# A list scheduler that ranks operations by their own index, against one that passes over the program forwards and backwards

## The chip, the cores and the metric

The kernel runs on one core of one Trainium2 chip. The metric is the device time of one execution in microseconds (us), the median of several runs. The core has five engines that each run their own instructions in the order in which the program issues them: TensorE (PE, matrix multiplies; its weight loads show as PEld), VectorE (DVE), ScalarE (ACT), GpSimd (POOL) and SyncE (SP, which here only issues DMA transfers). They wait for each other by semaphores.

## What is computed

Top-k attention over 4 batches of 8 heads (576 tokens, 64 columns a head), followed by two feed-forward stages on the 2304 tokens:

```python
scores = scale * np.matmul(q, k.transpose(0, 1, 3, 2))
kth = np.partition(scores, -top_k, axis=-1)[..., -top_k:-top_k + 1]   # top_k = 32
scores = np.where(scores >= kth, scores, -1000000000.0)
attn = np.exp(scores - np.max(scores, axis=-1, keepdims=True))
attn = attn / (np.sum(attn, axis=-1, keepdims=True) + 1e-09)
x = np.matmul(attn, v)            # then heads beside each other: 2304 x 512
h = x @ w_in                      # 512 -> 2048
x = (h * (1.0 / (1.0 + np.exp(-h)))) @ w_out
x = ((x @ w1) * (x @ w2) @ w3) @ w_out2   # 512 -> 1024 -> 1024 -> 512
```

## The kernel before

The tokens are worked in six blocks of 384 (three tiles of 128 each). For a block, attention goes head by head. PE makes the scores (`bank<-kk,qs`), ACT copies them out of the PSUM bank (`st<-bank`), DVE finds the 32 largest of each row in four rounds of `max` with three of `match_replace` between them (`top<-wk`, `wk<-top`), ACT masks and exponentiates (`e<-st,top`, `e<-e,nb`), DVE makes the reciprocal of the sum (`rc`), POOL multiplies (`e<-e,rc`), PE transposes (`bank<-ident,e`; in block 0 it multiplies by a diagonal instead, `dg`), ACT copies (`pn`, `pf`, `ph`), and PE multiplies with the values (`pn,vn`, `ph,vt`, `pl,vt`). When the eight heads of a block are done, its feed-forward work follows on PE: `xh,wt` and `gh,wt` with their low halves `xl` and `gl`, `x2h,wt`, and at the end `w4h,gh`. A matrix product in high precision is made of three PE products, since each operand is split into a rounded high half (ACT) and a rest (POOL subtracts). The gate of the first stage goes `th` (ACT), `gf` (DVE), `gh` (ACT), `gl` (POOL). All eight PSUM banks are one pool with the tag `bank`.

While block 0 and its feed-forward stage run, the weights are made ready: SP loads 48 pieces of 512 KB (`raw`), ACT, POOL and DVE unpack them (`t`, `bank<-raw,low`, `w`), ACT and POOL split them (`wt<-w`, `wt<-w,wt`), and ACT stores them to a scratch tensor in memory (`scr<-wt`), from which later blocks read them (`wt<-scr`). Ahead of that w3 and the last weight are multiplied with each other ("fold", `bank<-w`, `bank<-w4r,w`), so that one product is left of the two.

The order of the instructions is not written out. Every call is recorded as an `Op` with what it needs; `Op.cost` gives each a modelled time on its engine (`hold`) and until its result is there (`done`), in ns. `Recorder.schedule` then lets the five engines run in that model: whenever an engine is free it takes, among the operations whose inputs and buffers are there, the one with the lowest index in the recorded program. Sorted by the modelled start, the calls are issued by `emit` (L356 in the profile: all engine instructions have this one line, so the rows are read by their tiles). Buffers of a pool are handed out in the recorded order of their first use.

Of the kernel before, what the change touches and what calls it, by code (L numbers as in the profile page):

```python
# [2 lines left out]

# [11 lines left out]
I16 = mybir.dt.int16  # L15
# [124 lines left out]
class Op:  # L140
# [63 lines left out]
class Recorder:  # L204
# [52 lines left out]
    def schedule(self):  # L257
        ops = self.ops
        left, heirs, weak = [len(o.needs) + len(o.weak) for o in ops], [[] for _ in ops], [[] for _ in ops]
        users, ahead, turn = {}, {}, {}  # L260
        for n, o in enumerate(ops):
            for k in sorted(o.needs):
                heirs[k].append(n)
            for k in sorted(o.weak):
                weak[k].append(n)
            for t in o.tiles:
                users[t] = users.get(t, 0) + 1
            for t in o.takes:
                turn[t] = ahead[t.key] = ahead.get(t.key, -1) + 1
        spare = {k: [(0., c) for c in range(v)] for k, v in self.caps.items()}  # L270
        given, lastuse, parked = {}, {}, {}
        avail, start = [0.] * len(ops), [0.] * len(ops)
        ready = {e: [] for e in ("sync", "scalar", "vector", "gpsimd", "tensor")}
        later = {e: [] for e in ready}
        free = dict.fromkeys(ready, 0.)
        wire = busy = held = 0.
        reserved = {}

        def offer(n):
            o = ops[n]  # L280
            for t in o.takes:
                if t in reserved:
                    continue
                if given.get(t.key, 0) != turn[t] or not spare[t.key]:
                    parked.setdefault(t.key, []).append(n)
                    return
            for t in o.takes:
                if t not in reserved:
                    reserved[t] = heapq.heappop(spare[t.key])
                    given[t.key] = given.get(t.key, 0) + 1  # L290
                avail[n] = max(avail[n], reserved[t][0])
            heapq.heappush(later[o.engine], (avail[n], n))
            for t in o.takes:
                wake(t.key)

        def wake(key):
            for n in parked.pop(key, []):
                offer(n)

        for n in range(len(ops)):  # L300
            if not left[n]:
                offer(n)
        for _ in ops:
            best = None
            for e in ready:
                if ready[e] or later[e]:
                    t = free[e] if ready[e] else max(free[e], later[e][0][0])
                    if best is None or t < best[0]:
                        best = t, e
            t, e = best  # L310
            while later[e] and later[e][0][0] <= t:
                heapq.heappush(ready[e], heapq.heappop(later[e])[1])
            n = heapq.heappop(ready[e])
            o = ops[n]
            late = 0.
            if o.shares and busy > t + AVOID:
                aside = [n]
                while ready[e] and ops[ready[e][0]].shares:
                    aside.append(heapq.heappop(ready[e]))
                n = heapq.heappop(ready[e]) if ready[e] else aside.pop(0)  # L320
                for x in aside:
                    heapq.heappush(ready[e], x)
                o = ops[n]
            if o.shares:
                late = max(0., busy - t)
                held = t + late + o.hold
            elif e == "gpsimd":
                late = max(0., held - t)
                busy = t + late + o.hold
            start[n] = t  # L330
            free[e] = t + late + o.hold
            end = t + late + o.done
            if o.dma:
                wire = max(wire, t + 1400) + o.done
                end = wire + 1050
            for x in o.tiles:
                users[x] -= 1
                lastuse[x] = max(lastuse.get(x, 0.), end + 45)
                if not users[x]:
                    heapq.heappush(spare[x.key], (lastuse[x], reserved[x][1]))  # L340
                    wake(x.key)
            for k in heirs[n]:
                left[k] -= 1
                same = e == "tensor" and ops[k].engine == e
                avail[k] = max(avail[k], free[e] if same else end + 45)
                if not left[k]:
                    offer(k)
            for k in weak[n]:
                left[k] -= 1
                if not left[k]:  # L350
                    offer(k)
        return [ops[n] for n in sorted(range(len(ops)), key=lambda n: (start[n], n))]

    def emit(self):
        for o in self.schedule():
# [4 lines left out]
def attention_moe_moe2_kernel(  # L360
# [839 lines left out]
```

## Time and profile before

| | |
|---|---|
| median of 3 runs | 1139.78 us (1139.05 to 1140.88) |
| the profiled execution's own time | 1139.82 us |
| its span, first to last instruction | 1138.0 us |
| PE busy | 1081.0 us (95%) |
| DVE, ACT, POOL busy | 903.2, 854.9, 745.3 us |
| mean granted clock of TensorE | 0.983 of 2.4 GHz |

The span is what the trace covers; 1.8 us of the execution's time lie around it. Busy time is the union of an engine's instructions. The granted clock has two levels here, 1.0 (2.4 GHz) and 0.5 (1.2 GHz); a mean between them says how much of a stretch stood at each.

### The profile page before, as it was taken

Reading aid. Unit: us, or ns where it says so; the run is one execution under the profiler, and the core shown is the slowest. Engines: PE = TensorE matmul, PEld = TensorE weight load, DVE = VectorE, ACT = ScalarE, POOL = GpSimd, SP = SyncE. Lnnn points to the kernel's source line nnn. Section 1 sums busy time; section 2 is a strip of 40 time slices with the busy share of each in tenths; the row PEclk is TensorE's granted clock in tenths of the full one; section 3 lists DMA queues with packets and bytes.
Section 4 is the critical chain, followed back from the end, with each engine's and each line's share of the span. In section 5 each row is a group of like instructions: output and inputs, shape, how many; then the busy total and the mean of one; then the engine's idle time right before and its main releaser. Section 6 shows DMA issues by size and latency. Waiting matters only on the chain.

```text
span 1138.0 us, 19557 instructions
## 1 busy us (share of the span) xinstructions
PE 1081.0 (95%) x6096; PEld 986.9 (87%) x6096; DVE 903.2 (79%) x2062; ACT 854.9 (75%) x1911; POOL 745.3 (65%) x766
## 2 busy tenths in 40 slices
PE   3899977988899999999999999999999999999998
PEld 2555557888898999999999999999999999999997
DVE  7999899897989999998999888888899999401100
ACT  5999699898787778878887887888787778542221
POOL 3778458888786567777777866777766677542221
PEclk8999998999899999999999999999999999999999
DMA  8896389999988776767778667888757765448740
GB/s 263 263 288 197 114 271 308 313 324 315 313 290 290 231 238 216 238 205 231 253 259 292 222 200 275 272 306 296 253 171 254 252 226 192 136 158 259 254 146 29
DMA packets 127880, 273.54 MB, mean 240 GB/s; under 512 B 40480, under 2 KB 65056, under 8 KB 127776
## 3 DMA queue, kind: packets, MB, share of 16 engines
q1 hardware_dynamic: 119712, 245.02, 66.6%
q10 hardware_dynamic: 8064, 27.27, 6.2%
q8 instruction: 49, 0.80, 0.3%
q14 instruction: 55, 0.45, 0.1%
HBM read 216.14 MB, written 56.10 MB: 239 GB/s over the span
## 4 chain that ended last, share of the span: by engine, by line
PE 79%; ACT 7%; DVE 6%; POOL 3%; issue 3%; DMA 2%; ACTq 0%; SPq 0%; POOLq 0%; DVEq 0%
PE bank L356 79%; DVE top L356 3%; DVE wk L356 2%; ACT e L356 2%; POOL gl L356 1%; ACT t L356 1%; ACT st L356 1%; DVE w L356 1%; ACT wt L356 1%; ACT bank L356 1%; POOL wt L356 1%; ACT pn L356 1%; DMA raw<-in_w_dram 1%; DMA kk<-k 0%; DMA wt<-scr 0%
## 5 line engine op out<-in xcount | busy, mean ns | idle before, releaser
L356 DVE MAX8 top<-wk 128x8 f32<-128x576 f32 x432 | 319.9, 753 | 5.3
L356 POOL TENSOR_TENSOR gl<-gf,gh 128x384 fp32r<-128x384 f32 x144 | 147.2, 1022 | 158.8 <-ACT gh L356 157.6
L356 PE MATMUL bank<-xh,wt 128*128 128x384 f32 x768 | 225.0, 344 | 7.7 <-ACT st L356 7.0
L356 PE MATMUL bank<-gh,wt 128*128 128x384 f32 x768 | 224.9, 343 | 3.7 <-ACT gh L356 3.5
L356 PE MATMUL bank<-x2h,wt 128*128 128x384 f32 x768 | 221.7, 344 | 0.2 <-ACT x2h L356 0.2
L356 DVE MATCH_REPLACE8 wk<-top,wk 128x576 f32<-128x576 f32 x288 | 213.3, 742 | 0.0
L356 PE MATMUL bank<-kk,qs 128*128 128x288 f32 x640 | 150.8, 322 | 21.8 <-ACT kk L356 15.2
L356 ACT ACTIVATE st<-bank 128x288 f32<-128x288 f32 (+1 forms) x320 | 129.3, 411 | 39.8 <-PE bank L356 36.7
L356 POOL TENSOR_TENSOR pl<-pf,ph 128x384 fp32r<-128x384 f32 x128 | 129.5, 1018 | 38.0 <-ACT ph L356 35.8
L356 PEld LDWEIGHTS bank<-kk,qs 128*128 128x128 f32 x640 | 116.3, 195 | 41.1 <-issue 18.6
L356 PEld LDWEIGHTS bank<-xh,wt 128*128 128x128 f32 x768 | 142.9, 190 | 10.1 <-ACT st L356 7.7
L356 PEld LDWEIGHTS bank<-gh,wt 128*128 128x128 f32 x768 | 141.4, 190 | 5.1 <-ACT gh L356 4.7
L356 PEld LDWEIGHTS bank<-x2h,wt 128*128 128x128 f32 x768 | 141.6, 189 | 2.6 <-ACT x2h L356 0.8
L356 PE MATMUL bank<-gl,wt 128*128 128x384 f32 x384 | 131.4, 342 | 2.4 <-POOL gl L356 1.9
L356 DVE MAX8 top<-st 128x8 f32<-128x576 f32 x144 | 108.0, 752 | 29.2 <-ACT st L356 28.4
L356 PE MATMUL bank<-xl,wt 128*128 128x384 f32 x384 | 130.5, 340 | 0.0
L356 PE MATMUL bank<-x2l,wt 128*128 128x384 f32 x384 | 129.9, 339 | 0.1
L356 POOL TENSOR_SCALAR e<-e,rc 128x640 f32<-128x640 f32 (+1 forms) x120 | 95.6, 805 | 35.5 <-DVE rc L356 32.9
L356 ACT CAST gh<-gf 128x384 fp32r<-128x384 f32 x144 | 74.1, 515 | 52.7 <-DVE gf L356 51.5
L356 ACT ACTIVATE e<-st,top 128x576 f32<-128x576 f32 x144 | 107.4, 778 | 6.6 <-DVE top L356 5.3
L356 ACT ACTIVATE e<-e,nb 128x576 f32<-128x576 f32 x144 | 111.6, 777 | 0.0
L356 DVE SCALAR_TENSOR_TENSOR gf<-th,bank 128x384 f32<-128x384 f32 x96 | 52.5, 547 | 74.2 <-ACT th L356 72.5
(82 smaller groups left out, 2333.1 us busy)
## 6 DMA issues: line engine op xcount, KB each, us to landing
wt<-scr SPq DMA_DIRECT2D x240, 512.0 KB, 4.2
scr<-wt ACTq DMA_DIRECT2D x48, 512.0 KB, 5.3
k<-kk SPq DMA_DIRECT2D x32, 576.0 KB, 4.2
kk<-k SPq DMA_DIRECT2D x32, 576.0 KB, 5.0
raw<-in_w_dram SPq DMA_DIRECT2D x24, 512.0 KB, 5.7
kr<-in_kT_dram SPq DMA_DIRECT2D x32, 288.0 KB, 4.8
raw<-in_w3T_dram SPq DMA_DIRECT2D x16, 512.0 KB, 5.1
raw<-in_w_in_dram SPq DMA_DIRECT2D x16, 512.0 KB, 6.0
```

Source lines behind the costliest of these rows:

```text
L356: o.call(*[real_ap(x) for x in o.args], **{k: real_ap(x) for k, x in o.kw.items()})
```

## The change

Three things are different; the operations, their number and their sizes are not.

The times in `Op.cost` are set anew for a few kinds: matmuls 2 ns longer or 14 ns shorter, POOL's multiply and subtract by other straight lines, ACT's copies that don't read a bank 29 ns longer. The delay from a result to the instruction that waits for it, 45 ns for all before, is 17 to 70 ns by the waiting engine (`WAKE`).

The forward pass takes a rank in place of the recorded index. `backward` runs the same model from the end: an operation may start (backwards) when all that use its result have, buffers are taken at their last use and come free at their first, and the modelled place from the end is the new rank, so that an operation that may run late has a high one.

`schedule` begins with the recorded index as the rank, and then makes 24 rounds of two passes each, forwards and backwards, with durations that are disturbed at random by up to 5% (transfers by up to 15%). It keeps the rank whose forward passes in three fixed sets of disturbed durations have the least modelled end. The last forward pass uses the plain durations.

```diff
+ROUNDS = 24
+CASES = 3
+ENGINES = ("sync", "scalar", "vector", "gpsimd", "tensor")
+WAKE = (17, 24, 24, 70, 44)
+POOL, PE = 3, 4
...
-                t = max(m / 2.4 * 13 / 12, 110)
+                t = max(m / 2.4 * 13 / 12 + 2, 110)
-                t = 108 if self.name == "transpose" else m / 0.6 + (100 if columns(src) < 128 else 20)
+                t = 108 if self.name == "transpose" else m / 0.6 + (100 if columns(src) < 128 else 6)
...
-                t = 740 if src.dtype == I16 else max(360, n * 1.14 + 45)
+                t = 740 if src.dtype == I16 else n * 0.85 + 236
             else:
-                t = n * 2.42 + 46
+                t = n * 2.16 + 146 if n > 64 else 300
         if self.name == "copy":
-            t = n / 0.96 - 24
+            t = n / 0.96 + (-24 if in_bank(self.ins) else 5)
...
+    def forward(self, rank, hold, done):
+        ops, engine = self.ops, self.engine
+        left = [len(o.needs) + len(o.weak) for o in ops]
+        offer, back, pick, avail, free = self.queues(rank, self.takes, self.turn, left, lambda n: 0.)
+        users, lastuse = [len(u) for u in self.users], [0.] * len(self.key)
+        start, total = [0.] * len(ops), 0.
+        wire = busy = held = 0.
+            t, e, ready = pick()
+            n = heapq.heappop(ready)[1]
...
+            total = max(total, end)
...
+        return start, total
+
+    def backward(self, start, hold, done):
+        ops, engine = self.ops, self.engine
+        last = [max(u, key=lambda n: (start[n], n)) for u in self.users]
+        left = [len(h) for h in self.heirs]
+        takes, before, turn, seen = [[] for _ in ops], [[] for _ in ops], [0] * len(last), {}
+        for t in sorted(range(len(last)), key=lambda t: (-start[last[t]], -last[t], t)):
+            turn[t] = seen[self.key[t]] = seen.get(self.key[t], -1) + 1
+            takes[last[t]].append(t)
...
+        rank = [-(start[n] + hold[n]) for n in range(len(ops))]
+        offer, back, pick, avail, free = self.queues(rank, takes, turn, left, lambda n: done[n] - hold[n] + 45)
+        users, firstuse = [len(u) for u in self.users], [0.] * len(last)
+        begin, wire = [0.] * len(ops), 0.
+        for _ in ops:
+            t, e, ready = pick()
+            n = heapq.heappop(ready)[1]
+            free[e] = t + hold[n]
+            u = t + hold[n]
+            if ops[n].dma:
+                wire = max(wire, t) + done[n]
+                u = max(u, wire + 1400)
+            begin[n] = -u
...
+            for k in self.needs[n]:
+                left[k] -= 1
+                gap = 1050 if ops[k].dma else done[k] - hold[k]
+                avail[k] = max(avail[k], free[e] if e == PE and engine[k] == PE else u + gap + self.wake[n])
...
+        return begin
+
+    def jitter(self, dice, amount):
+        hold, done = [], []
+        for o in self.ops:
+            f = 1. + amount * (2. * dice.random() - 1.)
+            hold.append(o.hold if o.dma else o.hold * f + (0. if o.engine == "tensor" else 8.))
+            done.append(o.done * (1. + 3. * amount * dice.random()) if o.dma else o.done * f + 8.)
+        return hold, done
+
+    def schedule(self):
+        self.graph()
+        dice = random.Random(7)
+        cases = [self.jitter(dice, 0.04) for _ in range(CASES)]
+
+        def cost(rank):
+            return sum(self.forward(rank, *c)[1] for c in cases)
+
+        rank = list(range(len(self.ops)))
+        least = cost(rank)
+        for _ in range(ROUNDS):
+            times = self.jitter(dice, dice.choice((0., 0.02, 0.05)))
+            r = rank
+            for _ in range(2):
+                r = self.backward(self.forward(r, *times)[0], *times)
+                c = cost(r)
+                if c < least:
+                    least, rank = c, r
+        start, _ = self.forward(rank, [o.hold for o in self.ops], [o.done for o in self.ops])
+        return [self.ops[n] for n in sorted(range(len(start)), key=lambda n: (start[n], n))]
```

The instructions of an engine stay close to where they were: at the same place stand 4054 of PE's 5792, 837 of ACT's 1822, 702 of DVE's 1630, 327 of POOL's 758 and 355 of SP's 650; the mean distance is 2.1 places on PE and ACT, 1.4 on DVE and POOL, 0.9 on SP, and it is largest in the first third. Three places are shown, with the buffers' numbers, which differ between the two programs.

The first is ACT in the feed-forward stage of block 0, where the gate of its first piece of 128 columns goes from `th` to `gh` (`th_1881`, `gh_1924` before; `th_1838`, `gh_1863` after). Before:

```order
L356 ACTIVATE th_1881<-bank_1777 128x384
L356 DMA scr4_96<-wt_1851 128x1024
L356 ACTIVATE t_1885<-raw_1654 128x512
L356 ACTIVATE bank_1891<-raw_1654,low_90 128x512
L356 CAST wt_1899<-w_1807 128x512
L356 ACTIVATE t_1905<-raw_1682 128x512
L356 CAST wt_1911<-w_1871 128x512
L356 ACTIVATE st_1813<-bank_1819 64x288
L356 CAST qs_1915<-qr_1796 128x384
L356 CAST kk_1919<-kr_1856 128x576
L356 DMA scr5_97<-wt_1899 128x1024
L356 CAST gh_1924<-gf_1889 128x384
```

After:

```order
L457 ACTIVATE th_1838<-bank_1780 128x384
L457 ACTIVATE bank_1844<-raw_1639,low_90 128x512
L457 ACTIVATE st_1697<-bank_1765 128x288
L457 ACTIVATE st_1859<-bank_1822 128x288
L457 CAST gh_1863<-gf_1847 128x384
```

Before, ten instructions stood between the two (unpacking, splitting and storing of weights, a copy of scores, the casts `qs` and `kk` of a later head); now three do, a step of unpacking and two copies of scores.

The second is POOL a little ahead of it, where the low half of a head's queries is made (`qs_1775` before, `qs_1770` after, the sixth row and the last). Before:

```order
L356 TENSOR_TENSOR wt_1652<-w_1585,wt_1652 128x512
L356 TENSOR_SCALAR t_1665<-t_1665 128x512
L356 TENSOR_TENSOR wt_1687<-w_1614,wt_1687 128x512
L356 TENSOR_SCALAR t_1721<-t_1721 128x512
L356 TENSOR_TENSOR wt_1729<-w_1658,wt_1729 128x512
L356 TENSOR_TENSOR qs_1775<-qr_1551,qs_1775 64x384
L356 TENSOR_SCALAR e_1746<-e_1746,rc_1772 128x576
L356 TENSOR_SCALAR e_1750<-e_1750,rc_1772 128x576
L356 TENSOR_TENSOR kk_1780<-kr_1573,kk_1780 128x576
L356 TENSOR_TENSOR xl_1847<-xf_1693,xh_1802 128x384
L356 TENSOR_SCALAR t_1830<-t_1830 128x512
L356 TENSOR_TENSOR wt_1851<-w_1691,wt_1851 128x512
```

After:

```order
L457 TENSOR_TENSOR xl_1663<-xf_1364,xh_1657 128x384
L457 TENSOR_SCALAR dg_1468<-ident_89,rc_1655 128x128 x2
L457 TENSOR_SCALAR t_1674<-t_1674 128x512
L457 TENSOR_SCALAR t_1718<-t_1718 128x512
L457 TENSOR_TENSOR wt_1734<-w_1641,wt_1734 128x512
L457 TENSOR_TENSOR wt_1744<-w_1711,wt_1744 128x512
L457 TENSOR_SCALAR t_1748<-t_1748 128x512
L457 TENSOR_TENSOR kk_1758<-kr_1636,kk_1758 128x576
L457 TENSOR_TENSOR xl_1794<-xf_1691,xh_1785 128x384
L457 TENSOR_TENSOR qs_1770<-qr_1497,qs_1770 64x384
```

The subtraction for `qs` has moved behind those for a later `kk`, `xl`, a `t` and a `wt`, which followed it before; the two multiplications `e` that came right after it have gone further back too.

The third is the end of the program on PE. `bank_14016`, `bank_14024` and `bank_14032` collect the last block's three output tiles in this order, and each is copied out by ACT when its last product is done. Before, the last nine products:

```order
L356 MATMUL bank_14016<-w4h_87,gh_14289 128x512
L356 MATMUL bank_14016<-w4l_88,gh_14289 128x512
L356 MATMUL bank_14016<-w4h_87,gl_14293 128x512
L356 MATMUL bank_14024<-w4h_87,gh_14289 128x512
L356 MATMUL bank_14024<-w4l_88,gh_14289 128x512
L356 MATMUL bank_14024<-w4h_87,gl_14293 128x512
L356 MATMUL bank_14032<-w4h_87,gh_14289 128x512
L356 MATMUL bank_14032<-w4l_88,gh_14289 128x512
L356 MATMUL bank_14032<-w4h_87,gl_14293 128x512
```

After, rows up to six ahead of the end:

```order
L457 MATMUL bank_14016<-w4h_87,gh_14280 128x512
L457 MATMUL bank_14016<-w4l_88,gh_14280 128x512
L457 MATMUL bank_14016<-w4h_87,gl_14284 128x512
L457 MATMUL bank_14032<-w4h_87,gh_14203 128x512
L457 MATMUL bank_14032<-w4l_88,gh_14203 128x512
L457 MATMUL bank_14032<-w4h_87,gl_14207 128x512
L457 MATMUL bank_14024<-w4h_87,gh_14248 128x512
L457 MATMUL bank_14024<-w4l_88,gh_14248 128x512
L457 MATMUL bank_14024<-w4h_87,gl_14253 128x512
L457 MATMUL bank_14032<-w4h_87,gh_14248 128x512
L457 MATMUL bank_14032<-w4l_88,gh_14248 128x512
L457 MATMUL bank_14024<-w4h_87,gh_14280 128x512
```

The first tile's products are now finished (`gl_14284` into `bank_14016`) with fifteen products of the others still to come, where six came behind it before.

## Rows read from the trace of the kernel before

**Rows 1.** The page: span, and busy time of PE, DVE, ACT, POOL.

```profile
span 1138.0 us, 19557 instructions
PE 1081.0 (95%) x6096; PEld 986.9 (87%) x6096; DVE 903.2 (79%) x2062; ACT 854.9 (75%) x1911; POOL 745.3 (65%) x766
```

**Rows 2.** Windows: length, busy us by engine (instructions), granted clock, DMA share, GB/s.

```profile
0.00:69.30 69.30, 46.29 (x185) 29.36 (x185) 60.45 (x140) 54.73 (x118) 39.51 (x44) 0.90 0.84 266
69.30:142.00 72.70, 72.70 (x290) 42.62 (x290) 68.30 (x165) 60.49 (x129) 48.49 (x53) 1.00 0.59 186
142.00:313.00 171.00, 145.23 (x787) 130.26 (x785) 154.30 (x328) 151.10 (x320) 137.18 (x134) 0.93 0.92 308
171.00:199.00 28.00, 21.60 (x109) 20.02 (x108) 27.01 (x56) 25.63 (x54) 23.06 (x23) 0.82 0.90 307
142.00:342.00 200.00, 174.23 (x951) 157.33 (x950) 179.31 (x380) 176.41 (x374) 161.09 (x156) 0.94 0.91 305
199.00:285.00 86.00, 76.17 (x430) 71.11 (x429) 72.81 (x157) 75.51 (x158) 75.85 (x72) 0.96 0.94 317
342.00:967.00 625.00, 621.95 (x3764) 600.23 (x3763) 567.26 (x1321) 507.01 (x1176) 442.65 (x461) 1.00 0.74 244
967.00:1138.00 171.00, 165.86 (x914) 157.38 (x912) 27.89 (x60) 56.23 (x118) 53.57 (x54) 1.00 0.50 163
```

**Rows 3.** Timeline of PE: start, us, what, idle before and what ended it.

```profile
69.27 0.53 PE L356 MATMUL bank<-kk,qs 128*128 128x288 f32 x2 [1.74 <-ACT st L356]
...
155.78 0.71 PE L356 MATMUL bank<-dg,e 128*128 128x128 f32 x4 [2.03 <-POOL dg L356]
...
168.74 0.54 PE L356 MATMUL bank<-kk,qs 128*128 128x288 f32 x2 [1.25 <-POOL qs L356]
...
178.06 0.33 PE L356 MATMUL bank<-ident,e 128*128 128x128 f32 x1 [3.70 <-POOL e L356]
180.56 0.69 PE L356 MATMUL bank<-gh,wt 128*128 128x384 f32 x1 [2.16 <-ACT gh L356]
...
229.76 0.69 PE L356 MATMUL bank<-xh,wt 128*128 128x384 f32 x1 [4.09 <-ACT st L356]
...
244.42 0.55 PE L356 MATMUL bank<-ident,e 128*128 128x128 f32 x3 [1.65 <-ACT pn L356]
...
277.70 0.69 PE L356 MATMUL bank<-xh,wt 128*128 128x384 f32 x1 [2.94 <-ACT st L356]
...
298.15 0.61 PE L356 MATMUL bank<-kk,qs 128*128 128x288 f32 x1 [2.05 <-ACT x2h L356]
```

**Rows 4.** Waits of SP's queue between 100 and 142 us: total, times, longest.

```profile
SPq L356 <- PE bank L356: 20.1, 3, 18.4
```

**Rows 5.** Timeline of ACT around 227 us.

```profile
227.20 0.62 ACT L356 CAST wt<-w 128x512 fp32r<-128x512 f32 x1 [3.23 <-DMA kk<-k]
...
229.33 0.38 ACT L356 ACTIVATE st<-bank 64x288 f32<-64x288 f32 x1
```

**Rows 6.** Groups of POOL by form: count, busy us, mean ns, idle before.

```profile
L356 POOL TENSOR_TENSOR wt<-w,wt 128x512 fp32r<-128x512 f32 x48 | 63.2, 1320 | 14.3 <-ACT wt L356 11.7 <-DVE nb L356 0.4 <-PE bank L356 0.4
L356 POOL TENSOR_SCALAR t<-t 128x512 int16<-128x512 int16 x72 | 59.5, 826 | 31.9 <-ACT t L356 25.2 <-PE bank L356 1.9
L356 POOL TENSOR_TENSOR kk<-kr,kk 128x576 fp32r<-128x576 f32 x31 | 44.4, 1431 | 13.7 <-ACT kk L356 12.4
L356 POOL TENSOR_TENSOR xl<-xf,xh 128x384 fp32r<-128x384 f32 x8 | 8.1, 1014 | 2.6 <-ACT xh L356 2.2 <-PE bank L356 0.2
```

**Rows 7.** Timeline of POOL: the `qs` of the second place.

```profile
167.69 1.00 POOL L356 TENSOR_TENSOR qs<-qr,qs 64x384 fp32r<-64x384 f32 x1 [4.34 <-DVE rc L356]
```

**Rows 8.** Timeline of the end: PE's last product, ACT's three copies.

```profile
1132.71 0.40 PE L356 MATMUL bank<-w4h,gl 128*128 128x512 f32 x1
...
1131.73 1.29 ACT L356 COPY o<-bank 128x512 f32<-128x512 f32 x2 [1.69 <-PE bank L356]
1134.48 0.59 ACT L356 COPY o<-bank 128x512 f32<-128x512 f32 x1 [1.46 <-DMA out_dram<-o]
```

More of the change, by code (lines that the diff above doesn't have):

```diff
@@ L255, in add, with graph @@
             log.append((r, n, write))
-    def schedule(self):
+    def graph(self):
         ops = self.ops
-        left, heirs, weak = [len(o.needs) + len(o.weak) for o in ops], [[] for _ in ops], [[] for _ in ops]
-        users, ahead, turn = {}, {}, {}
+        self.needs = [sorted(o.needs) for o in ops]
+        self.heirs, self.after = [[] for _ in ops], [[] for _ in ops]
+        index, self.key, self.turn, ahead = {}, [], [], {}
+        self.users, self.takes = [], [[] for _ in ops]
@@ L261, in schedule @@
         for n, o in enumerate(ops):
-            for k in sorted(o.needs):
-                heirs[k].append(n)
+            for k in self.needs[n]:
+                self.heirs[k].append(n)
             for k in sorted(o.weak):
-                weak[k].append(n)
-            for t in o.tiles:
[L267 to L277, printed above, removed]
-        def offer(n):
[L280 to L294, printed above, removed]
@@ L296, in wake @@
-        def wake(key):
-            for n in parked.pop(key, []):
-                offer(n)
-        for n in range(len(ops)):
+                self.after[k].append(n)
+            for t in o.takes:
+                index[t] = len(self.key)
+                self.takes[n].append(index[t])
+                self.turn.append(ahead.get(t.key, 0))
+                ahead[t.key] = ahead.get(t.key, 0) + 1
+                self.key.append(t.key)
+                self.users.append([])
+            for t in o.tiles:
+                self.users[index[t]].append(n)
@@ new lines, in graph, with queues, wake, back @@
+        self.tiles = [[index[t] for t in o.tiles] for o in ops]
+        self.engine = [ENGINES.index(o.engine) for o in ops]
+        self.wake = [WAKE[e] for e in self.engine]
+    def queues(self, rank, takes, turn, left, gap):
+        given, spare = dict.fromkeys(self.caps, 0), {k: [0.] * c for k, c in self.caps.items()}
+        got, parked, avail = [None] * len(self.key), {}, [0.] * len(self.ops)
+        later, ready, free = [[] for _ in ENGINES], [[] for _ in ENGINES], [0.] * len(ENGINES)
+        key, engine = self.key, self.engine
+        def offer(n):
+            more = {}
+            for t in takes[n]:
+                if got[t] is None:
+                    k = key[t]
+                    x = more.get(k, 0)
+                    if given[k] + x != turn[t] or len(spare[k]) <= x:
+                        parked.setdefault(k, []).append(n)
+                        return
+                    more[k] = x + 1
+            for t in takes[n]:
+                if got[t] is None:
+                    got[t] = heapq.heappop(spare[key[t]])
+                    given[key[t]] += 1
+                if got[t] > 0.:
+                    avail[n] = max(avail[n], got[t] + gap(n))
+            heapq.heappush(later[engine[n]], (avail[n], rank[n], n))
+            for t in takes[n]:
+                wake(key[t])
+        def wake(k):
+            for n in parked.pop(k, []):
+                offer(n)
+        def back(t, when):
+            heapq.heappush(spare[key[t]], when)
+            wake(key[t])
+        def pick():
+            when = None
+            for e in range(len(ENGINES)):
+                t = free[e] if ready[e] else max(free[e], later[e][0][0]) if later[e] else None
+                if t is not None and (when is None or t < when):
+                    when, at = t, e
+            while later[at] and later[at][0][0] <= when:
+                _, r, n = heapq.heappop(later[at])
+                heapq.heappush(ready[at], (r, n))
+            return when, at, ready[at]
+        for n in range(len(self.ops)):
@@ L301, in schedule @@
             if not left[n]:
                 offer(n)
-        for _ in ops:
[L304 to L314, printed above, removed]
+        return offer, back, pick, avail, free
@@ L321, in schedule @@
                 for x in aside:
-                    heapq.heappush(ready[e], x)
-                o = ops[n]
-            if o.shares:
+                    heapq.heappush(ready, (rank[x], x))
+            if ops[n].shares:
                 late = max(0., busy - t)
-                held = t + late + o.hold
-            elif e == "gpsimd":
+                held = t + late + hold[n]
+            elif e == POOL:
                 late = max(0., held - t)
-                busy = t + late + o.hold
+                busy = t + late + hold[n]
@@ L339, in schedule @@
                 if not users[x]:
-                    heapq.heappush(spare[x.key], (lastuse[x], reserved[x][1]))
-                    wake(x.key)
-            for k in heirs[n]:
+                    back(x, lastuse[x])
+            for k in self.heirs[n]:
                 left[k] -= 1
-                same = e == "tensor" and ops[k].engine == e
-                avail[k] = max(avail[k], free[e] if same else end + 45)
+                avail[k] = max(avail[k], free[e] if e == PE and engine[k] == PE else end + self.wake[k])
@@ L346, in schedule @@
                 if not left[k]:
                     offer(k)
-            for k in weak[n]:
+            for k in self.after[n]:
                 left[k] -= 1
```

38 lines of the change are left out of this document (27 added, 11 removed).

## The prediction

> **What bounds the kernel now.** I read the page first: PE is busy for 1081.0 of 1138.0 us, DVE for 903.2 [rows 1]. A change of order alone can therefore win back at most what PE idles, 57 us, plus what it loses at the lower clock. The second view is the windows, to see where that is [rows 2]. From 342 to 967 us PE is busy 621.95 of 625 us, and from 967 to 1138 us 165.86 of 171. There is nothing to win there but the last few us. From 69.3 to 142 us PE has no gap at all. What is left is 0 to 69.3 us with 23.0 us idle, and 142 to 313 us with 171.00 - 145.23 = 25.8 us idle. In this second stretch no engine is full (DVE 154.3, ACT 151.1, PE 145.2 of 171), but the DMA engines are: their share is 0.92, and 0.94 from 199 to 285 us. This is where weights are loaded, unpacked and stored while block 0's feed-forward stage already uses them, so PE waits now for one engine and now for another. The third view is PE's timeline in this stretch, for the waits one by one [rows 3]. Since behind 342 us PE is full and its order is nearly the same, whatever the program reaches earlier at 342 us should arrive at the end in full.
>
> **What the change costs and saves.** No instruction is added or removed, so the sum is made of waits that go, come or stay, against the profiled execution's own 1139.82 us (span 1138.0 plus 1.8; the median of the runs is 1139.78, the same within their scatter).
>
> *The start, up to 69.3 us.* The long waits for the second head's keys and for the fold's first weights have the same releasing instructions at the same places on ACT and POOL, so I take nothing for them (bounds 0 and a fraction of a us either way). The wait of 1.74 us at 69.27 is for a copy of scores that stood on ACT behind two pairs of `e` [rows 3]; it now stands nine places further ahead, in front of all four, while the matmul that waits for it moves only four. I take all of it: **1.7 us**. It is passed on, since PE then runs without a gap to 142 us, and SP's queue stands still for 18.4 us up to 139.3 us until PE is done with a bank or a buffer [rows 2, 4], so the next loads of weights are issued that much earlier too. Lower bound 0, if another wait replaces it.
>
> *142 to 342 us, PE's side.* Five of the waits have a releasing instruction that moves ahead on its engine against the PE instruction that waits. At 180.56 us PE waits 2.16 us for `gh`, which had ten instructions between `th` and itself and now has three (the first place of the order); `gh` moves 16 places ahead, PE's product three. At 229.76 us PE waits 4.09 us for a copy of scores; ACT had stood still for 3.23 us ahead of a `wt` cast, with that copy and a `th` queued behind it [rows 5], and now both stand ahead of the cast. At 244.42 us it waits 1.65 us for `pn`, now ten places ahead on ACT, as are PE's own transposes; a place on PE is 174.23 / 951 = 0.18 us here, one on ACT 176.41 / 374 = 0.47 [rows 2], so `pn` gains more. At 277.70 us it waits 2.94 us for a copy queued behind a `th` that needs a buffer from `gl`; this `gl` moves six places ahead on POOL. At 298.15 us it waits 2.05 us for `x2h`, now eight places ahead. Together 2.16 + 4.09 + 1.65 + 2.94 + 2.05 = 12.9 us [rows 3]. Three waits go the other way, all for POOL. `qs` (1.25 us at 168.74) now has a `kk`, an `xl`, a `t` and a `wt` more ahead of it (the second place): 1.43 + 1.01 + 0.83 + 1.32 = 4.6 us [rows 6], and its matmul moves back by only three places, 0.5 us, so up to 4.1 us more. The `e` of 178.06 us stands behind two more `wt`, two `t` and a `gl` (taken as 1.0, like `xl`), 5.3 us, but PE's transposes stand fifteen places later, 2.7 us: up to 2.6. `dg` (155.78) has a `kk` and an `xl` more ahead of it, 2.4 us, against four places or 0.7 us on PE: up to 1.7. The sum is between 0 and 8.4 us of loss. What speaks for the low end is that POOL was idle for 4.34 us just ahead of `qs` [rows 7], so that what is now ahead of it may run in that gap. PE's side gives 12.9 less 0 to 8.4, and with the middle, 4.2, it is 8.7 us.
>
> *142 to 342 us, the transfers' side.* The share of the DMA engines is 0.91 over these 200 us [rows 2], 182 us of work that the change doesn't lessen. At the 0.94 that they hold from 199 to 285 us it would take 182 / 0.94 = 193.6 us, which saves 6.4; at a full 1.00 it saves 18; at the share of now, nothing. SP's order helps a little: most raw loads of weights from 142 us on are one to four places ahead of before, and loads and stores of keys behind them. The smaller of the two sides decides, and I take **6.4 us**, since a share that was held for 86 us can be held for 200, and nothing shows a higher one.
>
> *342 to 1130 us.* PE idles some 3 us of 625; I take nothing.
>
> *The end.* The three output copies on ACT share two buffers. The last started at 1134.48, 1.46 us of idling after the second, when the first tile's transfer had landed; PE was done at 1132.71 + 0.40 = 1133.11 [rows 8]. With the first tile finished fifteen products ahead of the end, not six (the third place), its copy and transfer start about 9 x 165.86 / 914 = 1.6 us earlier [rows 2], and the last copy can follow PE's last product at about 1133.15: 1134.48 - 1133.15 = **1.3 us**. What could undo it is a wait for the last `gl`, which the reordering needs earlier; the stage before it is moved ahead by nine products for that, so I keep 1.3, with 0 as the bound.
>
> The sum is 1139.8 - 1.7 - 6.4 - 1.3 = **1130.4 us**, 0.8% less.
>
> **A rule against the row: the clock.** From 171 to 199 us the granted clock is 0.82 in the mean, so a third of that window stood at 1.2 GHz, behind the two longest waits in it (3.70 and 2.16 us); over 142 to 313 us it is 0.93 [rows 2, 3]. The work not done is 0.07 x 171 = 12.0 us at the full clock. The Trainium skill, "TensorE: Matmul & The Clock Gate", section "Part 1: The HAM clock gate", has it that the gate halves the clock when the array has been idle and gives it back when it has been kept busy; the drop behind these waits agrees. By that rule each wait removed gives back its slow stretch too, PE's side would be 12.9 + 12.0 = 24.9 us, and the sum 1139.8 - 1.7 - 24.9 - 1.3 = 1111.9 us. The row of the DMA engines does not allow it: 182 us of transfers don't fit into 200 - 24.9 = 175.1 us. So the clock enters only as a rival, cut off at a full DMA share.
>
> **Rivals.**
>
> *PE's waits decide, not the transfers.* If the loads spread into the calmer stretches on both sides (share 0.59 before 142 us, 0.74 after 342), all of 12.9 comes and none of POOL's loss: 1139.8 - 1.7 - 12.9 - 1.3 = 1123.9 us. With the clock given back, up to the 18 us of a full share, 1118.8. Against it: SP stands still up to 139.3 us as before, so the loads can't start much earlier.
>
> *The transfers absorb everything.* If the weights come at the pace of before, each wait that goes comes back at the next piece of weights, the stretch to 342 us keeps its length, the 1.7 us ahead of it included, and only the end's 1.3 is left: 1138.5 us, no change that can be told. For it: a share of 0.92 already. Against it: the share is 0.90 from 171 to 199 us and 0.94 right behind, so the pace isn't set by the DMA engines alone.
>
> *Slower: POOL's queue.* If POOL has no time for the instructions moved ahead of `qs`, `e` and `dg`, PE waits 8.4 us more at these three places, and if the transfers absorb the rest, 1139.8 + 8.4 - 1.3 = 1146.9 us. It decides from about 3.6 us of loss on, where it exceeds the end's gain by 0.2%. For it: all three instructions move further back on POOL than what waits for them moves on PE. Against it: POOL is busy for only 137.18 of 171 us in this stretch [rows 2].
>
> *The change does nothing.* 4054 of PE's 5792 instructions stand where they stood, and 24 rounds may only find what the model rewards. That ends where the second rival does, and shares its chance.
>
> **The numbers.** A measurement of this kernel can tell about 0.2%, 2.3 us, from no change. I give the forecast, with what lies around it (1126 to 1136), 0.50; PE's waits deciding (1118 to 1126) 0.15; the transfers absorbing it 0.20, of which 0.17 ends within 2.3 us of before and 0.03 just below; POOL's queue 0.15. Faster by over 0.2% is 0.50 + 0.15 + 0.03 = 0.68, the same 0.17, slower 0.15. The range of 1120 to 1140 leaves out the full clock gain below, and POOL's case and the upper edge of no change above, together not quite 0.2.
>
> **What would show it.** In the changed kernel's profile the idle time of PE from 142 to 313 us should be near 16 us, not 25.8; the waits for `gh` near 180 us, for scores near 230 and 278, for `x2h` near 298 gone or under 1 us; the DMA share over the stretch 0.94 and not 0.91; the point from which PE is full 8 us earlier; the last `o` copy within 0.2 us of PE's end. The forecast is wrong if new waits for POOL's `qs` or `e` of 2 us and more stand between 150 and 200 us, if the DMA share stays and the stretch keeps its length, or if PE is no longer full behind 342 us.

## The result, and the profile after

The changed kernel takes 1129.06 us (median of 4 runs, 1127.77 to 1130.65) against 1140.18 us for the kernel before (4 runs): a ratio of 0.9904 with an interval of 0.9887 to 0.9921, or 11 us less. The profiled execution, at 1130.65 us the longest of the four, has a span 9.2 us shorter than before's. The forecast was 9.4 us.

The page after, for [rows 1]:

```profile
span 1128.8 us, 19547 instructions
PE 1080.0 (96%) x6096; PEld 983.9 (87%) x6096; DVE 898.1 (80%) x2062; ACT 851.6 (75%) x1911; POOL 745.1 (66%) x766
```

The windows after, for [rows 2]; the last three rows are the stretches right behind two of PE's longest waits:

```profile
0.00:69.30 69.30, 50.10 (x185) 31.52 (x186) 59.02 (x139) 52.45 (x115) 36.60 (x42) 0.95 0.81 256
69.30:142.00 72.70, 71.96 (x282) 41.45 (x281) 72.14 (x171) 62.80 (x134) 51.90 (x57) 1.00 0.63 201
142.00:313.00 171.00, 148.33 (x822) 130.92 (x822) 154.52 (x331) 150.48 (x322) 135.91 (x133) 0.96 0.88 298
142.00:342.00 200.00, 176.27 (x976) 156.21 (x976) 176.25 (x380) 174.67 (x373) 160.68 (x157) 0.97 0.88 300
342.00:967.00 625.00, 623.54 (x3785) 603.85 (x3784) 568.50 (x1332) 510.93 (x1187) 446.51 (x464) 1.00 0.75 246
...
222.90:225.90 3.00, 3.00 (x10) 3.00 (x11) 3.00 (x7) 3.00 (x8) 1.55 (x2) 0.53 0.81 241
226.00:230.00 4.00, 4.00 (x26) 4.00 (x25) 2.89 (x9) 3.16 (x7) 3.58 (x5) 1.00 1.04 352
278.60:282.00 3.40, 3.40 (x20) 3.34 (x21) 3.40 (x8) 3.11 (x7) 1.90 (x2) 1.00 0.93 294
```

PE gained in two places. From 142 to 313 us its idle time is 171.00 - 148.33 = 22.7 us, where it was 25.8, and 822 of its instructions start there instead of 787. From 342 to 967 us, where I had expected nothing, 3785 start instead of 3764: 21 of them at 625 / 3764 us each are 3.5 us. The mean granted clock from 142 to 313 us rose from 0.93 to 0.96. The share of the DMA engines from 142 to 342 us fell from 0.91 to 0.88.

PE's timeline after, for [rows 3]:

```profile
35.27 0.85 PE L457 MATMUL bank<-kk,qs 128*128 128x288 f32 x2 [3.80 <-ACT st L457]
...
67.88 0.83 PE L457 MATMUL bank<-kk,qs 128*128 128x288 f32 x2
...
181.33 0.63 PE L457 MATMUL bank<-ident,e 128*128 128x128 f32 x2 [4.55 <-ACT st L457]
...
222.90 0.82 PE L457 MATMUL bank<-kk,qs 128*128 128x288 f32 x2 [3.68 <-issue]
...
278.59 0.44 PE L457 MATMUL bank<-xh,wt 128*128 128x384 f32 x1 [2.55 <-ACT st L457]
...
296.38 0.44 PE L457 MATMUL bank<-x2h,wt 128*128 128x384 f32 x1 [1.08 <-ACT wt L457]
```

From 142 to 313 us none of the waits that are not shown is over 2.0 us. Two of those shown, at 222.90 and 278.59 us, come right behind a standstill of ACT. ACT's timeline after, for [rows 5] (ACTq is ACT's issuing of a transfer):

```profile
217.37 0.51 ACT L457 CAST gh<-gf 128x384 fp32r<-128x384 f32 x1
220.56 0.33 ACTq L457 DMA_DIRECT2D scr<-wt  x1
220.99 0.71 ACT L457 ACTIVATE bank<-raw,low 128x512 int32<-128x512 uint32 x1 [3.10 <-DMA raw<-in_w_out_dram]
...
273.09 0.68 ACT L457 ACTIVATE t<-raw 128x512 f32<-128x512 f32 x1
276.75 0.33 ACTq L457 DMA_DIRECT2D scr<-wt  x1
277.12 0.71 ACT L457 ACTIVATE bank<-raw,low 128x512 int32<-128x512 uint32 x1 [3.35 <-POOL e L457]
```

`gh` ends at 217.88, and then nothing starts on ACT until the store `scr<-wt` has gone out at 220.56; the same from 273.76 to 276.75. Before, the same two stores stood from 223.96 to 226.83 (its row [rows 5] is the cast behind it, with `kk<-k` as what ended the wait) and from 275.02 to 276.48. The trace's records tell what they stood for. All 706 transfers of the program signal their end on one of only eight semaphores, 88 or 89 on each, and the store's instruction waits on the one that it is to signal itself. The order of the changed kernel on ACT, with the waits of each instruction (DMAHW0 to DMAHW7 are the eight), has it at 217.88 us as the second row:

```
387 L457 CAST gh_2417<-gf_2357 128x384
388 L457 DMA scr16_108<-wt_2384 128x1024 [waits DMAHW3_49,Pool_49]
389 L457 ACTIVATE bank_2430<-raw_2345,low_90 128x512 [waits DMAHW2_49,Activation_49]
```

That wait ends when the earlier transfer on this semaphore has landed, although the store uses nothing of it. After, it was a `raw` load that landed at 220.48, 0.08 us ahead of the store, and a load of `vn` that landed at 276.67; before, a `kk<-k` that landed at 226.75 and a `vn` at 276.40. Everything behind the store on ACT waits with it. For PE's wait at 278.59 the profile names ACT's `st`. For the one at 222.90 it names nothing, but DVE's reading of a bank ends 0.1 us ahead of it, and that had waited for the `th` that is the second instruction behind the store on ACT; in the program this product of PE waits for the signal of just this `gf`, whose bank it writes next:

```profile
222.25 0.56 DVE L457 SCALAR_TENSOR_TENSOR gf<-th,bank 128x384 f32<-128x384 f32 x1 [2.90 <-ACT th L457]
```

In the traces of e1, e6, e7, e9 and e11, which have the same order there, PE starts again 0.10 to 0.11 us behind this `gf` too.

The end, PE and then ACT, for [rows 8]:

```profile
1124.75 0.40 PE L457 MATMUL bank<-w4h,gl 128*128 128x512 f32 x1
...
1124.24 0.59 ACT L457 COPY o<-bank 128x512 f32<-128x512 f32 x1 [1.98 <-PE bank L457]
1125.23 0.59 ACT L457 COPY o<-bank 128x512 f32<-128x512 f32 x1 [0.40 <-PE bank L457]
```

The last copy starts 0.08 us behind PE's end at 1125.15, where it was 1.37 us behind before.

Where the time came from is seen by the start of PE's instructions, counted through (the two orders differ, so one such difference is good to a us or two; from the 300th to the 500th it lies between 1.6 us early and 1.5 us late): the 500th starts 0.8 us later than before, the 1500th (356.8 us before) 4.4 us earlier, the 3800th 8.0, the last one 8.0, and the span ends 9.2 us earlier.

### The profile page after: what moved, and what is told of

Its sections match the earlier page's. It is cut to its first block, busy times and chain, and to the rows that moved or that the text cites. A ratio compares the mean times of both kernels' runs of the same rounds, so it can differ in the third digit from the quotient of the medians.

```text
span 1128.8 us, 19547 instructions
## 1 busy us (share of the span) xinstructions
PE 1080.0 (96%) x6096; PEld 983.9 (87%) x6096; DVE 898.1 (80%) x2062; ACT 851.6 (75%) x1911; POOL 745.1 (66%) x766
## 4 chain that ended last, share of the span: by engine, by line
PE 63%; DVE 17%; ACT 9%; POOL 5%; issue 4%; DMA 1%; ACTq 0%; SPq 0%; POOLq 0%; DVEq 0%
PE bank L457 63%; DVE top L457 7%; DVE wk L457 6%; ACT e L457 3%; DVE gf L457 2%; POOL wt L457 1%; ACT st L457 1%; POOL gl L457 1%; POOL t L457 1%; POOL e L457 1%; ACT t L457 1%; ACT wt L457 1%; ACT pf L457 0%; DMA raw<-in_w_dram 0%; ACT ph L457 0%
## 5 line engine op out<-in xcount | busy, mean ns | idle before, releaser
L457 PE MATMUL bank<-xh,wt 128*128 128x384 f32 x768 | 221.4, 341 | 2.6 <-ACT st L457 2.6
L457 PE MATMUL bank<-gh,wt 128*128 128x384 f32 x768 | 221.9, 341 | 0.2 <-ACT gh L457 0.2
L457 PE MATMUL bank<-x2h,wt 128*128 128x384 f32 x768 | 217.3, 341 | 1.4 <-ACT wt L457 1.1
L457 PE MATMUL bank<-kk,qs 128*128 128x288 f32 x640 | 148.1, 321 | 21.8 <-ACT kk L457 12.0
```

What stands on the lines that cost most here:

```text
L457: o.call(*[real_ap(x) for x in o.args], **{k: real_ap(x) for k, x in o.kw.items()})
```

## The experiments

The ratios are to the kernel before, run beside them on the same chip (medians 1140.00, 1142.16 and 1139.86 us in the three groups, e1 to e4, e5 to e8, e9 to e12). Where a kernel has its order fixed, the table holds the numbers of the recorded operations:

```diff
-        for o in self.schedule():
+        for n in array.array("H", zlib.decompress(base64.b85decode("".join(ORDER)))):
+            o = self.ops[n]
```

**e1 and e2: either part of the order alone.** e1 has the order of after up to PE's instruction at 366 us and that of before from there, e2 the other way round (table as above).

> The order of the changed kernel up to the instruction of PE that starts at 366 us before, and the order of the kernel before from there. If the gain comes where the two traces part (theory): 4.4 us less than before, 1135.7 us, since PE's 1500th instruction starts 4.39 us earlier in the changed trace and the waits behind it come back. If the prediction's terms hold (1.7 and 6.4 us in front, 1.3 at the end): 8.1 us less, 1132 us.

> The order of the kernel before up to 366 us, and that of the changed kernel from there. Theory: the small waits at the passage from one block to the next, the x2 step of the last block and the last copy give the rest, 9.2 less 4.4 = 4.8 us, 1135.4 us. By the prediction's terms: only the last copy, 1.3 us, 1138.9 us. If the parts lean on each other (PE full behind 366 us only with the earlier start), the two halves together give less than 9 us.

e1: 1136.90 us, 0.9970 (0.9955 to 0.9985), 3.4 us less. e2: 1135.62 us, 0.9964 (0.9949 to 0.9979), 4.1 us less. In e1's trace PE's 1500th instruction is 4.7 us early, and 2.3 of that is lost between the 1600th and the 1700th, at the join of the two orders. In e2's it is 2.8 us late, with the very order of before up to there, and from it to the end of the span 4.5 us are won. So the gain is not all in the front: more than a third of it comes behind 366 us. The two parts together give 7.5 us, less than the 11 us of the whole order.

**e3 and e4: the new times alone, and the search alone.** e3 takes the new times and no rounds; e4 the rounds over the old times.

```diff
-ROUNDS = 24
+ROUNDS = 0
```

```diff
-WAKE = (17, 24, 24, 70, 44)
+WAKE = (45, 45, 45, 45, 45)
...
-                t = max(m / 2.4 * 13 / 12 + 2, 110)
+                t = max(m / 2.4 * 13 / 12, 110)
```

> The new times and delays of the model, with the recorded index as the rank (no rounds of the search). If the search makes the gain (theory): within 2 us of before. Rival, that the better fitted times make it: 1129 to 1132 us.

> The search of 24 rounds over the old times and the old delay of 45 ns for all engines. Theory, the search makes the gain with either set of times: 1127 to 1133 us. Rival, that it needs the better fitted times to find an order that holds on the chip: 1136 us or more.

e3: 1150.04 us, 1.0085 (1.0066 to 1.0105), 10 us more. e4: 1127.58 us, 0.9878 (0.9855 to 0.9902), which overlaps the change's own interval. The gain is that of the rounds; the new times by themselves lose, and show no gain under the rounds. Whether the backward rank brings it or the trying of 48 orders was not run apart. Of e3's loss, 7.4 us stand at PE's 1500th instruction, and the largest piece is again a store on ACT:

```profile
222.75 0.41 ACT L457 ACTIVATE st<-bank 128x288 f32<-128x288 f32 x1
229.00 0.33 ACTq L457 DMA_DIRECT2D scr<-wt  x1
229.37 0.49 ACT L457 ACTIVATE th<-bank 128x384 f32<-128x384 f32 x1 [6.21 <-DMA raw<-in_w_in_dram]
```

It stood for 5.84 us (223.16 to 229.00) until a `raw` load on the same semaphore had landed at 228.92, and PE waited 6.01 us, where the longest wait of this stretch before was 4.09:

```profile
230.41 0.69 PE L457 MATMUL bank<-xh,wt 128*128 128x384 f32 x1 [6.01 <-ACT xf L457]
```

**e5: one wait of the forecast alone.** The order of before, with only the `th` and the copy of scores of [rows 5] moved ahead of the store and the cast (table as above).

> The order of before with one place of it changed: at 224 us the copy of scores and the th that stood on ACT behind a store of weights and a wt cast now stand ahead of these two. The wait of 4.09 us at 229.76 us should be gone in the profile. If the waits of the stretch are worth what they show (the prediction's sum for PE's side): 3 to 4 us less, 1136 us. If the stretch gives such a wait back at the next tight place (theory, since 12.9 us of waits that the new order takes away shortened it by only 4): 0 to 1.5 us less.

1140.81 us, 0.9983 (0.9968 to 0.9998), 1.9 us less, near the second of the two expectations and half of the first; the profiled execution is 1.8 us longer than before's. The wait of 4.09 us at 229.76 is gone, and this stands 0.9 us later:

```profile
230.67 0.44 PE L680 MATMUL bank<-gl,wt 128*128 128x384 f32 x1 [3.85 <-POOL gl L680]
```

ACT, and then POOL, show why:

```profile
223.82 0.50 ACT L680 ACTIVATE th<-bank 128x384 f32<-128x384 f32 x1
224.43 0.40 ACT L680 ACTIVATE st<-bank 64x288 f32<-64x288 f32 x1
226.87 0.33 ACTq L680 DMA_DIRECT2D scr<-wt  x1
227.24 0.62 ACT L680 CAST wt<-w 128x512 fp32r<-128x512 f32 x1 [2.41 <-DMA kk<-k]
...
227.94 1.27 POOL L680 TENSOR_TENSOR wt<-w,wt 128x512 fp32r<-128x512 f32 x1 [2.73 <-ACT wt L680]
229.17 1.45 POOL L680 TENSOR_TENSOR gl<-gf,gh 128x384 fp32r<-128x384 f32 x1
```

The two moved instructions now run ahead of the store, but the store still goes out at 226.87 behind `kk<-k`, and the `wt` cast behind it on ACT is late as before. POOL waits 2.73 us for this cast, and the `gl` that PE needs is queued behind it on POOL. The wait was handed from one product to the next, by way of another engine.

**e6: fewer transfers.** After's order; of each of the 48 stores only half is written, and the loads read that half twice.

```diff
-            nc.scalar.dma_start(out=scr[a], in_=piece[0, a].bitcast(FP32))
+            nc.scalar.dma_start(out=scr[a][:, 1], in_=piece[0, a][:, 1].bitcast(FP32))
```

> The order of the changed kernel, with half of each of the 48 stores of weights left out (only the low halves are stored, 256 KB each, and later blocks read these twice, so that the weights of blocks 1 to 5 are not the real ones). That takes 12.6 of some 60 MB of transfers out of the stretch from 142 to 342 us. If the transfers set its length (the prediction's step): 10 us or more less, 1119 us. If they don't (theory, since the share fell to 0.88 in the changed trace while the stretch got shorter): within 2.5 us of 1129.

1126.53 us, 0.9859 (0.9833 to 0.9884). That is 0.45% or 5 us below after's ratio, where the profiled spans differ by 2.2 us; if the transfers' sum set the length, it should have been 10 us or more. After itself was not run again in the groups of e5 to e12, so they are set against it by way of the kernel before. The share of the DMA engines fell from 0.88 to 0.76:

```profile
142.00:342.00 200.00, 179.28 (x988) 159.22 (x988) 179.01 (x385) 176.69 (x379) 162.73 (x159) 0.96 0.76 248
```

In its trace PE keeps within 1.1 us of after's from the 300th to the 1100th instruction and is 2.6 us ahead from the 1200th on. Between them lies the second store, which now went out at 274.14 instead of 276.75; PE's wait of 2.55 us is gone.

**e7, e9, e10 and e11: less work for one engine each.** After's order; 24 instructions of DVE (17.8 us in after's trace), 20 of ACT (19.5), 24 of POOL (19.8) or 104 of PE (18.1) are not issued. The edit is of one kind (here POOL's; e9 also sets a factor in the step ahead of the one left out):

```diff
+            if n in self.skip:
+                continue
...
+        if LO <= n < HI + 12:
+            nc.skip.add(len(nc.ops))
         nc.gpsimd.tensor_scalar(top, top, 32767, FLOOR, op0=ALU.min, op1=ALU.max)
```

> The order of the changed kernel, with the third match_replace left out for 12 of the 72 pairs of tiles (those whose top-k lies between 148 and 340 us; the last eight of their 32 largest are then wrong). That takes 24 instructions of 742 ns, 17.8 us or 9%, off DVE in the stretch from 142 to 342 us. If DVE sets its length (theory: 18 of the 36 us of its chain in front of the full stretch are DVE's): 8 to 16 us less, 1113 to 1121 us. If the stretch is set by no engine alone: 2 to 6 us less.

> The order of the changed kernel, with the exponential left out for 10 of the 72 pairs of tiles (those whose top-k lies between 160 and 340 us; their attention weights are then wrong). That takes 20 instructions of 778 ns and their reads of the sum (197 ns), 19.5 us or 11%, off ACT in the stretch from 142 to 342 us. If ACT, which stood between the waits, sets the length of the stretch: 8 us or more less than the changed kernel, 1121 us. If no engine does alone (theory, from the 2 us that the same relief on DVE gave): 1 to 5 us less.

> The order of the changed kernel, with POOL's clipping step left out for 24 of the 48 pieces of weights (those unpacked between 205 and 300 us; weights at the ends of the range would then be wrong). That takes 24 instructions of 826 ns, 19.8 us or 12%, off POOL in the stretch. If POOL, the slowest step of each chain (1.0 to 1.4 us an instruction), sets the length: 8 us or more less, 1121 us. If no engine does alone (theory): 1 to 5 us less.

> The order of the changed kernel, with the second of three products (high weights by the low half of the data) left out 104 times in block 0's feed-forward stage, most of them between 166 and 270 us (block 0's output loses precision). That takes 104 x 0.174 = 18.1 us off PE in the stretch. If PE sets its length, as it does behind 342 us: 12 us or more less, 1117 us. If no engine does alone (theory): 1 to 5 us less.

| | us | ratio (interval) | ACT standing at stores, 142 to 342 us | PE at 352 us, against after |
|---|---|---|---|---|
| after | 1129.06 | 0.9904 (0.9887 to 0.9921) | 7.2 us | |
| e7, DVE | 1129.51 | 0.9886 (0.9863 to 0.9909) | 9.0 | -1.4 us |
| e9, ACT | 1130.47 | 0.9913 (0.9886 to 0.9940) | 9.7 | -1.3 |
| e11, PE | 1130.42 | 0.9915 (0.9889 to 0.9941) | 8.9 | -1.1 |
| e10, POOL | 1123.73 | 0.9851 (0.9822 to 0.9880) | 2.7 | -6.6 |
| e6, transfers | 1126.53 | 0.9859 (0.9833 to 0.9884) | 4.3 | -2.6 |
| before | | | 6.0 | +4.4 |
| e3, times alone | 1150.04 | 1.0085 (1.0066 to 1.0105) | 11.7 | +11.8 |
| e4, search alone | 1127.58 | 0.9878 (0.9855 to 0.9902) | 3.8 | -4.6 |
| e8, seed | 1132.74 | 0.9918 (0.9897 to 0.9940) | 3.7 | +1.0 |
| e12, longer search | 1121.67 | 0.9846 (0.9817 to 0.9876) | 7.5 | -4.2 |

The fourth column is added up from the traces: from the end of ACT's last instruction to the issue of the store, where that is over 0.1 us. It does not rank the kernels: the change itself lengthens it from 6.0 to 7.2 us, e8 with 3.7 is slower than e12 with 7.5. (e4's trace is of the fastest of its five runs, 1122.20 us.) So the change did not gain by it, and a standstill costs only where PE comes to wait for it. Some 18 to 20 us less for DVE, ACT or PE give no gain that these runs can tell, so none of the three paces the stretch in this order. For POOL it looks otherwise, but its trace gives another reason:

```profile
216.33 0.48 ACT L684 COPY xf<-bank 64x384 f32<-64x384 f32 x1
216.61 0.33 ACTq L684 DMA_DIRECT2D scr<-wt  x1
216.83 0.51 ACT L684 CAST gh<-gf 128x384 fp32r<-128x384 f32 x1
```

The store that stood for 2.67 us in after goes out without standing, because it signals another semaphore here, whose last transfer (`qr`) had landed at 214.06. The second also signals another one and stands for 0.5 us instead of 2.98. PE is 1.0 us ahead at the 800th instruction and 4.9 at the 850th, right behind the wait of 222.90; by the 900th 2.9 of that are lost again, so that it is 2.0 ahead; from the 1100th to the 1200th, around the wait of 278.59, it goes from 3.7 to 6.7, and stays there. So nearly half of the 6.6 us lies at the second store alone. The 1.0 us up to the 800th instruction and the 1.7 between the 900th and the 1100th lie away from both stores. The run changes POOL's load and the semaphores of five stores and seven loads at once, so it doesn't tell how much of the 6.6 is POOL's. In e7, e9 and e11 both stores still stand, the second for 5.04, 2.27 and 4.26 us: in e7 and e11 what reaches it earlier waits longer for the same landing.

**e8 and e12: another seed, and a longer search.** e8 is after with another seed. e12 is e4 with 150 rounds, its order fixed as a table.

```diff
-        dice = random.Random(7)
+        dice = random.Random(11)
```

```diff
-ROUNDS = 24
+ROUNDS = 150
```

> The changed kernel with another seed for the disturbed durations (11 in place of 7), so another order of the same quality by its model. If the gain is the search's (theory): 1126 to 1133 us. If this one order was lucky: within 3 us of before, 1140.

> The order that the search finds over the old times when it makes 150 rounds and not 24 (same seed). If more rounds find more of the same (theory): 1 to 4 us less than the 24 rounds over the old times, 1124 to 1127 us. Rival, that what is still to be had is inside the scatter of the stretch from 142 to 342 us: within 1 us of these.

e8: 1132.74 us, 0.9918 (0.9897 to 0.9940), which overlaps the change's interval, so the gain does not hang on one seed. e12: 1121.67 us, 0.9846 (0.9817 to 0.9876), faster than both kernels and than I had expected; its interval lies below the change's. It overlaps that of e4, so that 150 rounds bring more than 24 is not shown. Its windows:

```profile
142.00:342.00 200.00, 178.68 (x995) 160.63 (x994) 184.77 (x401) 178.50 (x383) 164.00 (x160) 0.96 0.90 308
342.00:967.00 625.00, 624.48 (x3803) 607.45 (x3802) 568.08 (x1331) 508.92 (x1182) 445.09 (x463) 1.00 0.75 246
```

In both stretches about 19 more of PE's instructions fit than in after. ACT still stands for 7.5 us at stores.

## Why the prediction was right, and where its steps were not

The total was right, 9.4 us against 9.2 in the traces and 11 by the medians. That is luck: three of its four terms were off, and their errors, 2.5 and 1.8 us too much and 3.5 too little, nearly cancel.

*The start, 1.7 us.* The wait at 69.27 is gone and its product stands at 67.88, as forecast. But PE was 1.8 us late ahead of it. At its 55th instruction, where it waited 3.56 us for the fold's first weights before, a pair of scores now waits 3.80 us at 35.27, and the clock behind it stays low for longer (0.85 in the mean from 35 to 57 us, 0.92 before). The 1.7 us only made up for this, and the 500th instruction is 0.8 us late. What failed is that I costed the waits of the start whose releasing instructions keep their places at nothing, and looked for no new one.

*142 to 342 us, PE's side.* Of the 12.9 us, the waits for `pn` (1.65) and `x2h` (2.05) are gone from their places, 3.7 us, with 1.08 us for a `wt` just ahead of the last. Near 180 us, where PE waited 3.70 us for `e` and then 2.16 for `gh`, the transposes now wait 4.55 us for a copy of scores on ACT, which shows no gap there from 173.84 us on: 1.3 us less in all. The 4.09 and 2.94 us at 229.76 and 277.70 are back as 3.68 and 2.55. I had read them as work queued ahead of a copy of scores; the records show the copy behind a store that stands for a landing, and the order changed only what is caught behind it (e5). At these two places something like the second rival was right, by which a wait that goes comes back at the next piece of weights; here it came back at the next store's landing. POOL's losses did not come: `qs` waits 0.5 us, `dg` not at all, and no product of this stretch over 1.2 us for `e`, as the gap in [rows 7] had suggested.

*142 to 342 us, the transfers' side.* This is the step that was wrong in kind: "the smaller of the two sides decides", with the share going to 0.94. It went to 0.88 while the stretch got shorter, and at 0.76 (e6) 2.6 us were won, at one landing that PE waited for. The share is no ceiling either: from 226 to 230 us after it reads 1.04, and from 69.3 to 80 us before it was 0.98, where I had seen nothing over 0.94. So not the sum of the transfers holds up the stretch; two of its three longest waits hang on single landings, and the longest, 4.55 us, on ACT's queue. What paces the rest of it stays open. It gave 4.6 us in the trace (from 0.8 late to 3.8 early at the 1400th instruction) instead of 6.4. PE's idle time from 142 to 313 us went down by 3.1, to 22.7 and not to 16; the clock's rise is another part, which was not told apart.

*The clock.* The granted clock rose from 0.93 to 0.96 over 142 to 313 us. Behind the wait of 3.68 us it is 0.53 for 3 us, near the lower level, and 1.00 from 226 us on; the products of that stretch start 0.32 us apart, and 0.17 us later. That agrees with the Trainium skill, "TensorE: Matmul & The Clock Gate", section "Part 1: The HAM clock gate", by which an idle array loses its clock. Behind the 4.55 us it is 0.51 from 181.3 to 184.3 us. But behind the 2.55 us at 278.59 it stays at 1.00 (the last row of the windows above), and before it was 0.56 behind the 2.94 us at the same place:

```profile
277.70:281.20 3.50, 3.50 (x12) 3.50 (x13) 3.01 (x7) 3.50 (x9) 2.74 (x3) 0.56 0.88 297
```

So a slow stretch went even where the wait stayed, and the two longest waits that stayed keep theirs; the case of 1111.9 us, which needs all of them gone, was out of reach without the DMA row too. I had let the clock in only as a rival.

*342 to 1130 us, taken as nothing.* It gave 3.5 us, and e2 shows it apart: 3.2 us from the 1500th instruction to the last. I had read 3 us of idle time as the most that could be won. But idle time counts only what lies between the modelled end of one product and the start of the next, and a product here lasts 0.33 us while the next one starts 0.17 us behind it. So a gap that shows as 0.35 us (at 467.18 before) puts the next start off by about 0.33 - 0.17 + 0.35 = 0.5 us. The idle time from 342 to 967 us went down by only 1.6 us. Counting instructions in a window, or comparing starts, measures it.

*The end, 1.3 us.* 1.37 less 0.08 is 1.29 us.

That the passes bring the gain and the new times do not (e3, e4) is no part of the forecast, which took the order as it stands. Why the order of e3 loses another 4 us behind 350 us was not looked into. That the standing at stores sets the waits at 222.90 and 278.59 is shown by the landing times and the rows behind them, and by e6, e10 and e5; a kernel that issues the stores from another queue, or on semaphores of their own, was not run, so what all of it is worth stays open. What e4 and e12 win besides is open too, since e12's stores stand as long as after's.

## What to carry to other kernels

Ahead of crediting a reorder with a removed wait, follow the queue of the releasing engine back to the first instruction that stood still: if that is the issue of a transfer, look at what it waits for, since moving the work around it can only hand the wait on (e5). Take what a nearly full engine can win from its starts, not from its idle time. Where a scheduler's model is imperfect, a search over it was worth more here than refitted times (e4 against e3).

## What the runs showed of the hardware that was not expected

A store's issue held ACT for 2.67 and 2.98 us (5.84 in e3) until an unrelated transfer on the same one of eight semaphores had landed. The waits stand in the program, so this is how it shares out semaphores and not a limit of the queue that the runs show; the planner's model holds the engine only for the issue itself.

Executions with one order differ by some microseconds: the 23 of the kernel before that were run beside e1 to e4 lie between 1136.21 and 1144.04 us. In the two traces that can be set against before's the difference arises in the first 350 us: with the order of before up to there, PE's 1500th instruction starts 2.8 us later in e2's trace, and with one small move 1.7 us later in e5's. Behind 370 us e5's stays 1.7 to 1.8 us late to the end. What varies in the front was not settled; the landings that ACT stands for are one candidate.
